# Filler from VectorE's zeros, batch 0's kv and raw products in halves, and a new order in an attention and gated-unit kernel

## The chip, the cores and the metric

The kernel runs on one core of a Trainium2 chip. The metric is the device time of one execution in microseconds; lower is better. A core has five engines with a queue each, and a queue runs in order: TensorE (PE, matrix products, with PEld for the loads of its stationary operand), VectorE (DVE), ScalarE (ACT), GpSimd (POOL) and SyncE (SP, which here only issues transfers). TensorE writes to PSUM, eight banks of 2 KB in each of 128 partitions; the other working memory is SBUF, and inputs and output lie in HBM, moved by 16 DMA engines. Steps on different engines are ordered by semaphores.

## The reference

Eight batches of linear attention (8 heads, 576 tokens, 64 wide) are followed by a gated unit with a causal convolution of five taps:

```python
kv = np.einsum('bhsd,bhse->bhde', k, v)
out = np.einsum('bhsd,bhde->bhse', q, kv)
rms = np.sqrt(np.mean(out * out, axis=-1, keepdims=True) + 1e-06)
out = out / rms * g_norm
x = out.transpose(0, 2, 1, 3).reshape(B, S, H * D)      # 8 x 576 x 512
for k in range(5):
    gate_pre += conv_w[k] * xp[:, k:k + S, :]            # xp: x with 4 rows of zeros ahead
gate = 1 / (1 + np.exp(-gate_pre))
return gate * (x @ w_val) @ w_out
```

q, k, v and `g_norm` are float32. The weights `w_val`, `conv_w` and `w_out` come as float64; the kernel reads them as pairs of 32-bit words and narrows them itself.

## The kernel before

**Plan and queues.** All work is cut into named steps (`kv_product 0 1` is half 1 of batch 0). A string, `PLAN`, holds some 1,235 of them in an order that a planner has written out; the program goes through it and issues each step's instructions, so the order of every engine's queue is the order of the plan, and so is SyncE's queue of transfers. Tiles come from pools: a PSUM bank is used again when its readers are done.

**Set-up.** `set_up` (L279) clears small tiles on VectorE (`warm`, biases, the whole of `kv_bd`) and makes the identity matrix on GpSimd (`make_identity`). `start_warm n` (L427) issues n filler products of 32 rows and columns, each of two instructions, that read the identity; nobody reads what they write.

**Batch 0 and 1, the opening.** Queries come in whole rows (`load_q_rows`, two transfers for a batch, one for each half of the heads), k and v in halves (`load_half`; batch 0's v on ScalarE's queue). `turn_q_rows b j` (L471) transposes four blocks of 32 tokens by products with the identity, and `sort_q` (L481) copies them from PSUM in the order of the heads. `kv_product b i` (L432) makes k'v for half i of the head pairs, 72 instructions of 64x64. For batch 0 alone `kv_copy` (L445) places the results as diagonal blocks in `kv_bd`, whose other blocks stay zero, so that a raw product `raw_whole 0 c` (L506) takes a chunk c of 128 tokens (chunk 4: 64) and two heads at once, 128x128. Its bank holds all four head pairs. Before, `kvps` of batch 0 is two banks, one for each s (the head within a pair's rows of k), both with two halves i; a copy step takes one bank and both halves, on ScalarE, and every raw product stands behind both copies.

**From raw to x.** `square` (ScalarE), `sums` (VectorE), `powers` (GpSimd, to the power -0.5) and `normalise` (batch 0: VectorE; others: ScalarE) give x; `turn_x` (TensorE) and `keep_x` (ScalarE), or from batch 2 on `turn_blocks` (VectorE) and `move_blocks` (transfers), transpose it into `xT`. `halo` (GpSimd) places the rows that the convolution needs.

**Gate, value, output.** `gate_start` (ScalarE), four `gate_tap` (VectorE), `gate_end` (ScalarE, sigmoid) and `gated` (VectorE) are the gate of one of four column blocks; `val_product`, or from batch 2 on `val_fast` with sums of blocks made ahead (seven products for eight), the value. `fast_product` does the same for the output matrix, with `token_sums` on VectorE; `out_product` takes the last 64 tokens of two batches at once. `store` writes the rows, `store_last` the last two blocks from two queues.

**Weights.** `stage_weight` loads float64 words; `narrow_weight name n part` has eight parts: 0, 5, 6, 4 and 7 on VectorE, 1, 2 and 3 on ScalarE. `cw`, the taps, is narrowed first, turned by `turn_cw` on TensorE and kept by `keep_cw`, whose `gcol` every `wval` needs in part 7. `warm_up` runs one sigmoid on ScalarE, which loads its table.

Of the kernel before, what the change touches and what calls it, by code (L numbers as in the profile page):

```python
# [15 lines left out]
P = 128  # L16
# [3 lines left out]
load_q_rows 0 1; stage_weight cw 0; load_q_rows 0 0; load_half v 0 0; load_half k 0 0; narrow_weight cw 0 5;  # L20
narrow_weight cw 0 6; narrow_weight cw 0 0; load_half v 0 1; load_half k 0 1; narrow_weight cw 0 1;
narrow_weight cw 0 2; warm_up; stage_weight wval 1; stage_weight wval 0; start_warm 36; turn_q_rows 0 3;
turn_q_rows 0 2; turn_q_rows 0 0; kv_product 0 0; turn_q_rows 0 1; sort_q 0 0; sort_q 0 1; narrow_weight cw 0 3;
narrow_weight cw 0 4; narrow_weight cw 0 7; turn_q_rows 0 4; turn_cw; keep_cw; kv_product 0 1; sort_q 0 4;
sort_q 0 3; kv_copy 0 0; kv_copy 0 1; narrow_weight wval 1 5; narrow_weight wval 1 0; sort_q 0 2; raw_whole 0 3;
load_q_rows 1 1; narrow_weight wval 1 1; narrow_weight wval 1 6; narrow_weight wval 1 2; raw_whole 0 4;
raw_whole 0 2; load_q_rows 1 0; narrow_weight wval 0 0; narrow_weight wval 0 5; square 0 3; stage_weight wval 3;
narrow_weight wval 0 6; narrow_weight wval 1 3; sums 0 3; load_half k 1 0; square 0 2; square 0 4;
narrow_weight wval 0 1; narrow_weight wval 1 4; sums 0 2; narrow_weight wval 0 2; raw_whole 0 0; raw_whole 0 1;
powers 0 3; sums 0 4; narrow_weight wval 1 7; normalise 0 3; square 0 1; square 0 0; sums 0 1; sums 0 0;  # L30
turn_q_rows 1 2; turn_q_rows 1 0; turn_q_rows 1 3; narrow_weight wval 0 3; sort_q 1 0; turn_x 0 3;
turn_q_rows 1 4; sort_q 1 2; turn_q_rows 1 1; keep_x 0 3; narrow_weight wval 3 0; load_half v 1 0;
stage_weight wval 2; load_half k 1 1; load_half v 1 1; powers 0 2; sort_q 1 3; normalise 0 2;
narrow_weight wval 3 1; narrow_weight wval 0 4; normalise 0 4; narrow_weight wval 0 7; narrow_weight wval 3 5;
stage_weight wout 1; load_q 2 0; stage_weight wout 0; powers 0 1; turn_x 0 4; narrow_weight wval 3 2;
turn_x 0 2; load_half k 2 0; kv_product 1 0; load_q 2 2; stage_weight wout 2; normalise 0 0; normalise 0 1;
narrow_weight wval 3 3; keep_x 0 2; keep_x 0 4; narrow_weight wval 3 4; narrow_weight wval 2 0; turn_x 0 0;
narrow_weight wval 3 6; turn_x 0 1; val_product 0 1 1; keep_x 0 0; kv_product 1 1; keep_x 0 1;
narrow_weight wval 3 7; narrow_weight wval 2 5; gate_start 0 0; val_product 0 3 1; gate_start 0 3;
narrow_weight wval 2 1; halo 0; sort_q 1 4; kv_copy 1 1; sort_q 1 1; kv_copy 1 0; gate_start 0 1;  # L40
narrow_weight wval 2 2; raw_pair 1 3; gate_tap 0 0 3; gate_tap 0 0 2; gate_tap 0 3 3; narrow_weight wval 2 3;
gate_tap 0 3 2; gate_tap 0 0 1; narrow_weight wout 1 0; narrow_weight wout 1 5; narrow_weight wval 2 6;
narrow_weight wval 2 4; load_half v 2 0; load_half k 2 1; load_q 2 1; square 1 3; narrow_weight wout 1 1;
narrow_weight wout 1 2; raw_tail 1; load_half v 2 1; keep_val 0 1 1; val_product 0 0 0; square 1 2;
narrow_weight wval 2 7; keep_val 0 3 1; gate_tap 0 3 1; sums 1 3; gate_tap 0 0 0; narrow_weight wout 0 0;
gate_tap 0 1 3; sums 1 2; turn_q 2 0; powers 1 3; keep_val 0 0 0; gate_end 0 0; val_product 0 2 1;
val_product 0 0 1; powers 1 2; load_q 2 3; narrow_weight wout 1 3; square 1 4; normalise 1 3; sums 1 4;
narrow_weight wout 1 6; narrow_weight wout 1 4; gate_tap 0 1 2; keep_val 0 0 1; val_product 0 1 0; raw_pair 1 1;
normalise 1 2; powers 1 4; turn_x 1 3; square 1 0; val_product 0 2 0; narrow_weight wout 1 7; gated 0 0;
gate_tap 0 1 1; keep_val 0 1 0; normalise 1 4; narrow_weight wout 0 1; sums 1 0; gate_start 0 2; turn_x 1 4;  # L50
turn_x 1 2; val_product 0 3 0; square 1 1; keep_x 1 4; keep_x 1 3; keep_x 1 2; narrow_weight wout 0 5;
gate_tap 0 3 0; val_sums 0; narrow_weight wout 2 5; narrow_weight wout 2 0; powers 1 0; gate_tap 0 2 3;
gate_tap 0 2 2; narrow_weight wout 0 2; gate_tap 0 2 1; sums 1 1; narrow_weight wout 0 3; keep_val 0 2 0;
keep_val 0 3 0; keep_val 0 2 1; stage_weight wout 3; narrow_weight wout 0 4; narrow_weight wout 0 6;
gate_tap 0 1 0; narrow_weight wout 2 6; gate_end 0 3; kv_product 2 0; normalise 1 0; powers 1 1;
val_product 1 0 1; halo 1; val_product 1 1 1; kv_product 2 1; turn_x 1 0; normalise 1 1; keep_val 1 0 1;
turn_q 2 2; narrow_weight wout 0 7; gate_tap 0 2 0; gate_end 0 1; gate_end 0 2; val_sums 1; turn_q 2 1;
gated 0 3; gated 0 2; turn_x 1 1; val_product 1 3 1; load_q 3 0; keep_x 1 0; turn_q 2 3; load_q 3 1;
load_half v 3 0; load_half v 3 1; narrow_weight wout 2 1; kv_copy 2 1; keep_x 1 1; weight_sums 0; val_sums 2;
gate_start 1 1; val_product 1 1 0; kv_copy 2 0; keep_val 1 1 1; narrow_weight wout 2 2; gate_tap 1 1 3;  # L60
keep_val 1 3 1; narrow_weight wout 2 3; narrow_weight wout 3 0; raw_pair 2 3; narrow_weight wout 3 5;
gate_tap 1 1 2; gated 0 1; square 2 2; square 2 3; keep_val 1 1 0; gate_start 1 0; narrow_weight wout 3 1;
raw_pair 2 1; val_product 1 0 0; narrow_weight wout 3 2; val_product 1 3 0; narrow_weight wout 3 3;
narrow_weight wout 3 6; token_sums 0 0 0; sums 2 3; val_product 1 2 1; val_product 1 2 0; powers 2 3; sums 2 2;
turn_q 3 0; token_sums 0 0 1; narrow_weight wout 3 4; square 2 1; keep_val 1 0 0; keep_val 1 3 0; load_q 3 3;
narrow_weight wout 3 7; narrow_weight wout 2 4; narrow_weight wout 2 7; load_half k 3 0; load_q 3 2;
load_half k 3 1; powers 2 2; fast_product 0 0 0; sums 2 1; normalise 2 3; token_sums 0 0 2; turn_blocks 2 3;
normalise 2 2; square 2 0; turn_q 3 1; powers 2 1; gate_start 1 3; fast_product 0 1 0; fast_product 0 0 1;
fast_keep 0 0 0; keep_val 1 2 0; normalise 2 1; weight_sums 1; raw_tail 2; sums 2 0; gate_tap 1 0 3;
fast_keep 0 0 1; fast_product 0 0 2; fast_keep 0 0 2; powers 2 0; square 2 4; keep_val 1 2 1; fast_keep 0 1 0;  # L70
weight_sums 2; token_sums 0 0 3; fast_product 0 0 3; fast_product 0 0 5; turn_blocks 2 2; turn_blocks 2 1;
sums 2 4; fast_keep 0 0 5; gate_tap 1 0 2; normalise 2 0; fast_product 0 0 4; fast_product 0 1 2; powers 2 4;
fast_keep 0 1 2; store 0 0; normalise 2 4; turn_blocks 2 0; move_blocks 2 0; move_blocks 2 2; move_blocks 2 1;
kv_product 3 0; fast_keep 0 0 4; turn_q 3 2; gate_tap 1 0 1; gate_tap 1 0 0; weight_sums 3; turn_q 3 3;
fast_product 0 1 4; turn_x 2 4; fast_product 0 1 1; kv_product 3 1; keep_x 2 4; kv_copy 3 0; kv_copy 3 1;
fast_product 0 0 6; move_blocks 2 3; raw_pair 3 3; raw_pair 3 1; gate_tap 1 3 3; load_half v 4 0; load_q 4 0;
gate_end 1 0; fast_keep 0 1 1; square 3 3; fast_keep 0 0 6; square 3 1; fast_product 0 1 3; fast_product 0 1 5;
gate_tap 1 3 2; gated 1 0; fast_keep 0 1 4; gate_tap 1 1 1; val_fast 2 0 0; sums 3 3; sums 3 1; gate_tap 1 1 0;
fast_keep 0 1 5; square 3 0; fast_product 0 1 6; square 3 2; sums 3 2; x_sums 2 0; gate_end 1 1; val_fast 2 1 0;
powers 3 3; x_sums 2 1; x_sums 2 3; gate_tap 1 3 1; gate_tap 1 3 0; val_fast 2 0 1; val_keep 2 0 0;  # L80
val_fast 2 0 2; x_sums 2 2; val_sums 3; sums 3 0; gated 1 1; fast_keep 0 1 6; val_keep 2 1 0; normalise 3 3;
val_keep 2 0 2; powers 3 2; powers 3 1; gate_end 1 3; val_fast 2 1 2; val_fast 2 1 1; load_half k 4 0;
val_keep 2 1 2; gate_start 1 2; val_keep 2 0 1; val_fast 2 0 4; gate_tap 1 2 3; val_keep 2 1 1; gate_tap 1 2 2;
val_fast 2 1 4; val_fast 2 0 5; val_fast 2 1 5; load_half v 4 1; normalise 3 2; load_half k 4 1; val_keep 2 0 4;
turn_blocks 3 2; val_keep 2 1 4; turn_q 4 0; val_keep 2 1 5; store 0 1; load_q 4 1; store 0 3; gate_tap 1 2 1;
# [122 lines left out]
def kernel(  # L208
# [11 lines left out]
    nc = tc.nc  # L220
# [628 lines left out]
```

## Time and profile before

| | |
|---|---|
| time, median of 3 runs | 306.39 us (304.39 to 307.18) |
| the profiled execution | 306.42 us |
| its span, first to last instruction | 304.6 us |
| TensorE busy | 294.8 us, 97% |
| VectorE busy | 269.2 us, 88% |
| ScalarE busy | 193.7 us, 64% |
| GpSimd busy | 114.9 us, 38% |
| mean granted clock of TensorE | 0.993 |
| moved by DMA | 55.53 MB, 182 GB/s in the mean |

All times below count from the first instruction of the span. A line such as L512 is a line of the kernel before. The granted clock is the share of TensorE's full clock that its throttle let through; its record starts 10.51 us into the span. The end of a product in a row is modelled and products overlap, so where rates matter the distance from one start to the next is used.

### The profile page before, as it was taken

What the parts mean: (1) busy time and instruction counts of PE and PEld (TensorE: products, weight loads), DVE (VectorE), ACT (ScalarE), POOL (GpSimd) and SP (SyncE); (2) the same over time, 40 slices, a digit from 0 to 9 for tenths busy, and PEclk for the clock granted to TensorE, in tenths of its full rate; (3) what the DMA queues carried; (4) which work ended last, traced back from release to release, by engine and by line L of the source; (5) the groups of instructions that cost most, each with busy time, mean ns of one, the idle gap of its engine ahead of it and who ended that gap; (6) DMA issues with size and microseconds to landing.
All of it is one profiled execution on the core that took longest, in us unless ns stands there. A gap on an engine that the chain in (4) does not pass through costs nothing.

```text
span 304.6 us, 8977 instructions
## 1 busy us (share of the span) xinstructions
PE 294.8 (97%) x3441; PEld 232.4 (76%) x3441; DVE 269.2 (88%) x474; ACT 193.7 (64%) x596; POOL 114.9 (38%) x127
## 2 busy tenths in 40 slices
PE   7899999999999999999999999999999999999993
PEld 7788778877787785777778757787878588888582
DVE  1169999999999999999999999999999999999612
ACT  1569989999768664884586547683787354535220
POOL 3027354406568217364338352345536631000000
PEclk9979999999999999999999999999999999999999
DMA  7999998088569756988689477927411621112423
GB/s 269 343 368 343 272 302 210 4 230 269 154 147 329 231 163 167 269 220 260 173 253 294 111 175 232 326 72 214 114 48 30 169 80 34 36 42 64 103 69 103
DMA packets 32074, 55.53 MB, mean 182 GB/s; under 512 B 6166, under 2 KB 14358, under 8 KB 32032
## 3 DMA queue, kind: packets, MB, share of 16 engines
q1 hardware_dynamic: 29520, 49.76, 55.7%
q0 software_dynamic: 1632, 3.17, 4.1%
q10 hardware_dynamic: 880, 2.03, 1.8%
q8 instruction: 27, 0.44, 0.6%
q14 instruction: 15, 0.12, 0.1%
HBM read 39.21 MB, written 9.44 MB: 160 GB/s over the span
## 4 chain that ended last, share of the span: by engine, by line
PE 89%; DVE 5%; DMA 2%; issue 1%; ACT 1%; DVEq 0%; ACTq 0%; SPq 0%
PE a L774 18%; PE cb L774 14%; PE va L682 13%; PE val L633 11%; PE vc L682 6%; PE kvps L440 6%; PE raw L501 5%; PE out L720 5%; PE vb L682 4%; PE qTps L477 4%; PE raw L512 2%; PE xTps L583 2%; DMA qs<-in_q_dram 2%; DVE gate L621 2%; DVE xs L667 1%
## 5 line engine op out<-in xcount | busy, mean ns | idle before, releaser
L552 POOL TENSOR_TENSOR rt<-ss,mhalf 128x8 f32<-128x8 f32 (+3 forms) x38 | 68.9, 1822 | 101.0 <-DVE ss L544 100.8
L621 DVE SCALAR_TENSOR_TENSOR gate<-xT,cwT,gate 128x576 f32<-128x576 f32 x128 | 101.8, 809 | 1.0
L571 ACT ACTIVATE x<-raw,rt 128x64 f32<-128x64 f32 x252 | 55.8, 351 | 7.2 <-POOL rt L552 4.2
L604 POOL DMA_DIRECT2D xT<-y x48 | 26.4, 557 | 25.5 <-DVE ot L784 14.0
L633 PE MATMUL val<-xT,wval 128*128 128x288 f32 x128 | 33.0, 411 | 0.0
L774 PE MATMUL a<-wsum,sums 128*128 128x256 f32 x128 | 32.4, 382 | 0.0
L628 ACT ACTIVATE gate<-gate 128x576 f32<-128x576 f32 x32 | 22.0, 692 | 11.7 <-DVE gate L621 11.4
L633 PEld LDWEIGHTS val<-xT,wval 128*128 128x128 f32 x128 | 23.5, 190 | 6.5 <-ACT xT L590 0.4
L544 DVE TENSOR_REDUCE ss<-sq 128x8 f32<-128x520 f32 (+1 forms) x40 | 24.7, 627 | 2.9 <-ACT sq L531 2.5
L774 PEld LDWEIGHTS a<-wsum,sums 128*128 128x128 f32 x128 | 24.0, 190 | 4.1 <-issue 0.6
L535 ACT ACTIVATE sq<-raw 128x256 f32<-128x256 f32 (+1 forms) x70 | 22.4, 403 | 7.3 <-PE raw L501 7.1
L682 PE MATMUL va<-xs,vsum 128*128 128x288 f32 x96 | 26.6, 409 | 0.0
L615 ACT ACTIVATE gate<-xT,cwT 128x576 f32<-128x576 f32 x32 | 25.2, 811 | 1.5 <-DVE gv L646 1.3
L646 DVE TENSOR_TENSOR gv<-gv,gate 128x576 f32<-128x576 f32 x32 | 23.6, 750 | 0.9 <-ACT gate L628 0.8
L682 PEld LDWEIGHTS va<-xs,vsum 128*128 128x128 f32 x96 | 18.0, 190 | 5.1 <-ACT x L571 0.4
L611 POOL COPY xT<-xT 128x124 f32<-128x124 f32 x32 | 17.5, 585 | 10.5 <-ACT xT L590 10.5
L501 PEld LDWEIGHTS raw<-kv,qT 64*64 64x64 f32 x1008 | 16.4, 134 | 5.3 <-issue 3.0
L440 PEld LDWEIGHTS kvps<-v,k 64*64 64x64 f32 x1008 | 15.9, 135 | 3.7 <-issue 1.9
L501 PE MATMUL raw<-kv,qT 64*64 64x64 f32 x1008 | 18.7, 221 | 0.0
L440 PE MATMUL kvps<-v,k 64*64 64x64 f32 x1008 | 17.6, 220 | 0.0
L774 PE MATMUL cb<-wsum,sums 128*128 128x256 f32 x64 | 16.9, 386 | 0.1
L774 PE MATMUL cb<-wout,gv 128*128 128x256 f32 x64 | 16.8, 385 | 0.0
(111 smaller groups left out, 542.3 us busy)
## 6 DMA issues: line engine op xcount, KB each, us to landing
qs<-in_q_dram SPq DMA_DIRECT2D x96, 140.0 KB, 4.2
out_dram<-ot SPq DMA_DIRECT2D x140, 64.0 KB, 1.7
k<-in_k_dram SPq DMA_DIRECT2D x14, 576.0 KB, 6.3
v<-in_v_dram SPq DMA_DIRECT2D x12, 576.0 KB, 6.5
xT<-y SPq DMA_DIRECT2D x48, 64.0 KB, 2.7
xT<-y POOLq DMA_DIRECT2D x48, 64.0 KB, 3.3
y<-in_moe_w_val_dram SPq DMA_DIRECT2D x4, 512.0 KB, 11.4
w_wout<-in_moe_w_out_dram SPq DMA_DIRECT2D x4, 512.0 KB, 6.3
```

The lines of the kernel that those rows point to most:

```text
L440: nc.tensor.matmul(st["kvps", b][s][r * D:(r + 1) * D, i], st["k", b, i][rows, r, cols], st["v", b, i][rows, r, cols], start=(j == 0), sto ...
L501: nc.tensor.matmul(st["raw", b, c][r][cols, to * D:(to + 1) * D], st["qT", b][rows, hp, first:first + D], kvs[b % 2][rows, hp, :], start=T ...
L544: nc.vector.reduce_sum(out=st["ss", b][:, FIRST[c]:FIRST[c] + n], in_=st["sq", b, c][:, 0:n], axis=AX.X)
L552: nc.gpsimd.tensor_tensor(out=st["rt", b][:, which], in0=st["ss", b][:, which], in1=mhalf[:, which], op=ALU.pow)
L571: nc.scalar.activation(out=x[:, to * D:(to + 1) * D], in_=raw[:, h * D:(h + 1) * D], func=AF.Copy, scale=root[:, to:to + 1])
L604: (nc.sync if i % 2 else nc.gpsimd).dma_start(out=xTs[b % 2][i * TB:(i + 1) * TB, :, first:first + P], in_=y[a * TB:(a + 1) * TB, i])
L615: nc.scalar.activation(out=gate[:], in_=xTs[b % 2][:, jt, HALO:SX], func=AF.Copy, scale=cwT[:, K - 1, jt:jt + 1])
L621: nc.vector.scalar_tensor_tensor(out=gate[:], in0=xTs[b % 2][:, jt, tap * TB:tap * TB + S], scalar=cwT[:, tap, jt:jt + 1], in1=gate[:], op ...
L633: nc.tensor.matmul(val[:], wval[:, kc, jt * P:(jt + 1) * P], xTs[b % 2][:, kc, HALO + n * SV:HALO + (n + 1) * SV], start=(kc == 0), stop=( ...
L646: nc.vector.tensor_tensor(out=both, in0=both, in1=st["gate", b, jt][:], op=ALU.mult)
L682: nc.tensor.matmul(st[bank, "val", b, mj][:], weights_[:, k], tokens()[:, k], start=(n in (0, 1, 3) and k == 0), stop=(k == NK // 2 - 1), ...
L774: nc.tensor.matmul(st[bank, i, p], tokens()[:, k], weights_[:, k], start=(n < 2 and k == 0), stop=(k == NK // 2 - 1), skip_group_check=True)
```

## The change

1. `set_up` clears the first 32 columns of `kv_bd` as VectorE's very first instruction and the rest of it later; `start_warm` reads those zeros instead of the identity, and the plan asks for 50 products (100 instructions) instead of 36 (72).
2. For batch 0, `kv_product` writes each half i and each s to a bank of its own: four banks instead of two. `kv_copy 0 n` copies half n alone, in four pieces of 64x64: the upper 64 partitions on ScalarE, the lower on VectorE. Before, a step made two pieces of 64x128 on ScalarE.
3. `raw_whole b c i` runs the two head pairs of half i alone, so that a half can run before the other half's kv is there. The products are the same in number and size.
4. The whole plan is new. Its opening, by name: the exponent of `cw` (part 0) is taken first and its part 3 stands right behind `warm_up`; TensorE runs query blocks 4, 0, 3, then kv half 0, query block 1, raw half 0 of chunk 3, `turn_cw`, query block 2, kv half 1, raw half 0 of chunk 2, and then the other raw halves; `load_q_rows 1` stands behind query block 2 (before: behind block 1, ahead of block 4); the `wval` narrowing on VectorE starts behind `kv_copy 0 1`.

```diff
     def set_up():
+        nc.vector.memset(kv_bd[:, 0, 0:TB], 0.0)
         nc.vector.memset(warm[:], 0.0)
...
         make_identity(nc, ident[:])
-        nc.vector.memset(kv_bd[:], 0.0)
+        nc.vector.memset(kv_bd[:, 0, TB:], 0.0)
+        nc.vector.memset(kv_bd[:, 1:], 0.0)
...
     def start_warm(n):
         for _ in range(n):
-            nc.tensor.matmul(warm_bank()[0:TB, 0, 0:TB], ident[:, 0:TB], ident[:, 0:TB], start=True, stop=True)
+            nc.tensor.matmul(warm_bank()[0:TB, 0, 0:TB], kv_bd[:, 0, 0:TB], kv_bd[:, 0, 0:TB], start=True, stop=True)
...
         if ("kvps", b) not in st:
-            st["kvps", b] = [ps([P, 2, D], f"kvps{b}_{s}") for s in range(2)]
+            whole = b in WHOLE
+            banks = [ps([P, 2 - whole, D], f"kvps{b}_{n}") for n in range(4 if whole else 2)]
+            st["kvps", b] = [[banks[2 * i + s][:, 0] if whole else banks[s][:, i] for i in range(2)] for s in range(2)]
+            st["kvbanks", b] = banks
...
-    def kv_copy(b, s):
-        ps_ = st["kvps", b][s]
+    def kv_copy(b, n):
         if b in WHOLE:
             for r in range(2):
                 rows = slice(r * D, (r + 1) * D)
-                nc.scalar.copy(
-                    out=kv_bd[rows, :, rows].rearrange("p (i s) e -> p s i e", s=2)[:, s], in_=ps_[rows])
+                for s in range(2):
+                    to, ps_ = kv_bd[rows, 2 * n + s, rows], st["kvps", b][s][n][rows]
+                    (nc.vector.tensor_copy if r else nc.scalar.copy)(out=to, in_=ps_)
             return
...
-    def raw_whole(b, c):
+    def raw_whole(b, c, i):
         m = size(c)
-        st["raw", b, c] = raw = ps([P, C if c < NJ else C // 2], f"raw{b}_{c}")
-        for hp in range(HP):
+        if ("raw", b, c) not in st:
+            st["raw", b, c] = ps([P, C if c < NJ else C // 2], f"raw{b}_{c}")
+        for hp in (2 * i, 2 * i + 1):
```

The plan before, its opening up to the second raw product (loads left out):

```
narrow_weight cw 0 5; narrow_weight cw 0 6; narrow_weight cw 0 0; narrow_weight cw 0 1; narrow_weight cw 0 2; warm_up;
start_warm 36; turn_q_rows 0 3; turn_q_rows 0 2; turn_q_rows 0 0; kv_product 0 0; turn_q_rows 0 1; sort_q 0 0;
sort_q 0 1; narrow_weight cw 0 3; narrow_weight cw 0 4; narrow_weight cw 0 7; turn_q_rows 0 4; turn_cw; keep_cw;
kv_product 0 1; sort_q 0 4; sort_q 0 3; kv_copy 0 0; kv_copy 0 1; narrow_weight wval 1 5; narrow_weight wval 1 0;
sort_q 0 2; raw_whole 0 3; ...; raw_whole 0 4; raw_whole 0 2
```

The plan after, the same stretch:

```
narrow_weight cw 0 0; narrow_weight cw 0 5; narrow_weight cw 0 1; narrow_weight cw 0 2; warm_up; narrow_weight cw 0 3;
start_warm 50; turn_q_rows 0 4; turn_q_rows 0 0; turn_q_rows 0 3; kv_product 0 0; turn_q_rows 0 1;
narrow_weight cw 0 6; narrow_weight cw 0 4; sort_q 0 0; sort_q 0 3; kv_copy 0 0; narrow_weight cw 0 7;
raw_whole 0 3 0; turn_cw; turn_q_rows 0 2; sort_q 0 2; keep_cw; kv_product 0 1; raw_whole 0 2 0; sort_q 0 4;
load_q_rows 1 0; load_q_rows 1 1; sort_q 0 1; kv_copy 0 1; narrow_weight wval 1 5; narrow_weight wval 1 0;
narrow_weight wval 1 6; raw_whole 0 3 1; raw_whole 0 4 0; raw_whole 0 4 1; raw_whole 0 2 1
```

## The prediction

> **What bounds the kernel now.** I read the page first, then the busy time by stretches, then TensorE's own row of time through the opening.
>
> The first part of the page and the stretches (columns: busy microseconds and instructions of TensorE, its weight loads, VectorE, ScalarE, GpSimd; granted clock; DMA share; GB/s):
>
> ```profile
> PE 294.8 (97%) x3441; PEld 232.4 (76%) x3441; DVE 269.2 (88%) x474; ACT 193.7 (64%) x596; POOL 114.9 (38%) x127
> ```
> ```profile
> 14.00:17.30 3.30, 1.69 (x74) 1.55 (x75) 2.49 (x9) 1.75 (x7) 0.00 (x0) 1.00 0.76 249
> 17.30:20.80 3.50, 3.50 (x18) 2.74 (x19) 1.91 (x5) 3.36 (x7) 0.00 (x0) 0.51 1.01 374
> ...
> 30.00:210.00 180.00, 179.36 (x2389) 139.26 (x2381) 178.51 (x307) 132.41 (x436) 82.40 (x89) 1.00 0.74 212
> 210.00:280.00 70.00, 69.79 (x506) 55.38 (x505) 67.27 (x109) 38.12 (x114) 22.48 (x27) 1.00 0.29 77
> ```
> Two engines are full from 30 to 280 us: TensorE is idle 0.85 us there, VectorE 1.49 + 2.73 us. So an opening that is shorter for one engine alone is worth nothing, and a re-planned middle has almost nothing left to win and all of that to lose. TensorE's order in time through the opening (start, length, line, product, count, idle before and its releaser):
>
> ```profile
> 1.36 4.05 PE L430 MATMUL warm<-ident 128*32 128x32 f32 x72 [1.36 <-POOL ident masks.py:199]
> 6.12 5.05 PE L477 MATMUL qTps<-ident,qs 128*64 128x128 f32 x48 [0.70 <-DMA qs<-in_q_dram]
> 11.10 1.28 PE L440 MATMUL kvps<-v,k 64*64 64x64 f32 x72
> 12.31 1.53 PE L477 MATMUL qTps<-ident,qs 128*64 128x128 f32 x24
> 15.05 0.21 PE L414 MATMUL cwps<-ident,cw 21*128 21x21 f32 x1 [1.22 <-issue]
> 15.19 1.40 PE L440 MATMUL kvps<-v,k 64*64 64x64 f32 x72
> 17.15 6.32 PE L512 MATMUL raw<-kvbd,qT 128*128 128x128 f32 x40 [0.56 <-ACT kvbd L450]
> 23.40 2.84 PE L477 MATMUL qTps<-ident,qs 128*64 128x128 f32 x48
> ```
> The same 48 query products take 105 ns each at 6.12 and 59 ns at 23.40: the clock was at half before 10.51, where its record begins (the stretches print 1.00 where there is no record). It fell to half once more, from 17.34 to 20.75, behind the idle 1.22 and 0.56 us: a stretch of 3.41 us that was busy 1.7 us, some 49%. The 40 raw products cost 6.25 us from start to start; the full-rate ones among them are 0.11 us apart, so 4.42 would do, and 1.83 us is the clock. Between 6.12 and 23.40 TensorE has 11.2 us of work at the full rate (72 query, 144 kv, 40 raw products): 6.1 us is there to be had.
>
> **The change part by part.**
>
> *Filler.* 72 instructions in 4.05 us are 54 ns each; 100 last 5.4. They wait for VectorE's first clear (first row at 0.81, some 0.06 long), not for GpSimd's identity at 1.36: from 0.95 to 6.3. The queries land at 6.07 and 6.25, so the 0.70 us gap closes and the work behind it is not delayed. Worth in time: nothing by itself, because of what follows. With the clock up early, the 40 query products (8 fewer now ahead of the first kv product) end at 8.7 and kv waits for its values, which land at 9.49; with it low they end at 10.5. kv half 0 and the query block behind it (1.21 + 0.94) end at 11.65 or 12.65. Both are too early for ScalarE:
>
> *ScalarE to the first kv copy.* The exponent of `cw` is taken first (L363 at 8.45, not 8.90), so its chain runs 0.45 earlier: two steps to 9.5, the table load 1.28 to 10.8, the sigmoid, the third step of `cw` to 11.4 (before it stood behind a query sort and ended at 14.33), two sorts (0.57 long, 0.48 apart) to 12.45, then the copies. A kv copy was 64x128 at 0.26; a 64x64 has no row, so its bounds are half of that, 0.13, and 0.26; I take 0.25, as a 21-column read of the same memory on VectorE (L419, 128x20) still took 0.24. VectorE's half has the same 0.25, bounds 0.15 and 0.41 (its 128x256 copy L797), and stands behind ScalarE's copy of the same bank. All four end at 13.2. All bounds move this by 0.5 either way.
>
> *First raw half and the rest.* Raw half 0 of chunk 3 runs at 13.2 for 0.44; `turn_cw` finds its input ready at 13.45 (not 15.02): 13.8; query block 2 to 14.75; kv half 1 (landed 13.80) to 15.95; raw half 0 of chunk 2 to 16.4. The second copies follow ScalarE's three sorts: 16.9. The other 32 raw instructions at 0.11 end at 20.5, against 23.40: 2.9 us for TensorE, 1.8 of it the clock. Splitting the raw products adds none.
>
> *What is queued behind.* On VectorE the first weight narrowing stood at 15.84; now it stands behind the second kv copies at 16.9. But from 15.84 to its first gate step at 33.11 it was idle 2.85 us (1.56 and 0.90 for squares, the rest in small pieces), so 14.4 us of work; the squares now come about 2 us earlier, and with no such wait the first gate step is at 31.3: 1.8 us earlier. On SyncE the batch 1 queries are now issued behind query block 2, 14.75 against 13.88, and with them nine transfers (two queries, four halves of k and v, two `wval`, one `wout`) some 0.85 later. Queries then land at 18.5 and 20.0 (were 17.61, 19.18), covered by 0.5 us; the first k and v halves of batch 1 at 26.3, needed at 27.2: covered.
>
> *TensorE to the first value product.* Two query blocks to 22.4; `turn_x 0 3` waits for its normalised chunk until 22.9 (sums 18.85, power 2.06, then six VectorE steps); the next query block waits for a bank that ScalarE frees behind three `wval` steps (0.7 each), until 24.65. From there rows of before: blocks 1.88, two turns 0.65, kv 1.21, block 0.47, two turns 0.95: the first value product at 29.85, against 31.16. So 1.3 us arrives on TensorE, 1.8 on VectorE.
>
> *The tail* has the same chain: the last product, a copy of 0.42, a store. Behind the last whole-bank product TensorE has 14 product steps of 0.86 us, before 13; the order ahead of it is one shorter, so the sum is unchanged unless VectorE is late there.
>
> Sum: the profiled execution took 306.42 us, its span 304.6; 306.42 - 1.3 = **305.1 us**. The median of the three runs shown is 306.39, so nothing is shifted.
>
> [...]
>
> **The rivals.**
>
> *The clock falls in a new wait (chance 0.22).* If the filler does lift the clock, TensorE idles from 11.65 to 13.2, and 10.51 to 13.93 is busy only 55%; from 20.75 to 24.17 it idles 0.5 and 0.8, 62%. Against it: 49% is the only share that is known to have dropped it, and the first stretches of filler, busy 68% and 79%, were low already. One fall in the first place makes 13.93 to 17.34 slow: query block and kv half 1 take 2.15 more, less the wait that this covers, some 1.2 late for both engines: 306.3. In the second, TensorE loses 1.5: 306.6.
>
> *VectorE late at the last batch (0.18, slower).* The place: `gated 7 0`, on which the last whole-bank product waits. Before, the gated rows ended at 283.77 and that product began at 284.41. Now TensorE would be there at 284.41 - 0.86 - 1.3 = 282.25, VectorE at 283.77 - 1.8 = 281.97, if its queue meets only the idle that it meets now. Each microsecond more than 0.28 is a microsecond of the end; slower than before from 1.6. If a wholly new order meets the idle of 30 to 280 us (4.2) twice: 306.42 - 1.3 + 3.9 = 309.0. For it: full engines and a strange order; against it: the counts of instructions are the same, and VectorE still has idle time after 210.
>
> *All of it arrives (0.20).* The whole 2.9 us of TensorE survives, because later waits fill behind stages that have slack: 303.5, and with luck in the middle 303. Against: VectorE gains 1.8 at best.
>
> *No filler effect at all* gives the forecast too, as shown.
>
> **How the numbers follow.** Forecast 305.1 with 0.40, between 304.2 and 306; clock 306.3 to 306.6 with 0.22; all arrives 303.5 with 0.20, half of it under 303.3; VectorE late 309.0 with 0.18, half of it above. One per cent is 3.06 us, which is also the spread of the runs shown (304.39 to 307.18) and about what a measurement can tell. So faster 0.10, same 0.81, slower 0.09. The range 303.0 to 308.7 leaves out about half of the last case and a third of the one before.
>
> **What would show it.** Filler from 0.95 to 6.3 and no gap before the query products; first raw product near 13.2, the last ending near 20.5 at 0.11 us spacing; the first weight narrowing near 16.9; the first value product near 29.9 and gate step near 31.3; no half clock between 14 and 27; VectorE idle 30 to 210 still under 2 us. Wrong it is if the clock drops again, if kv copies take over 0.4 us, or if VectorE idles in the middle.

## The result: 3.3% slower, and where the profile after has the time

The kernel after takes 315.75 us (median of 4 runs, 313.34 to 317.44); the kernel before, on the same chip, 305.39 us (304.08 to 307.18). The ratio is 1.0329, with a 95% interval of 1.0232 to 1.0426. The prediction was 305.1 us, the same within 1%, and its range ended at 308.7. It was wrong.

The profiled execution after took 313.34 us, the shortest of the four; its span is 311.6 us, 7.0 us more than the one before (304.6 us). The first part of its page, and the same stretches that were shown of the kernel before:

```profile
PE 296.5 (95%) x3469; PEld 233.5 (75%) x3469; DVE 270.0 (87%) x480; ACT 192.3 (62%) x596; POOL 113.5 (36%) x127
```
```profile
14.00:17.30 3.30, 3.30 (x96) 2.89 (x96) 1.29 (x7) 1.55 (x5) 0.00 (x0) 1.00 0.47 139
17.30:20.80 3.50, 3.50 (x36) 3.09 (x37) 3.47 (x9) 3.18 (x6) 1.78 (x1) 1.00 1.01 374
30.00:210.00 180.00, 173.78 (x2247) 135.19 (x2246) 170.49 (x292) 126.71 (x419) 78.81 (x81) 0.98 0.71 205
210.00:280.00 70.00, 69.50 (x582) 54.26 (x581) 66.72 (x108) 38.60 (x123) 23.44 (x30) 1.00 0.32 85
```

The two stretches of the opening have become what they were meant to be: TensorE busy throughout, at the full clock. The loss is in the third. There TensorE is idle 6.22 us (before 0.64) and VectorE 9.51 us (before 1.49). TensorE's own row of time through the opening:

```profile
0.96 5.32 PE L434 MATMUL warm<-kvbd 128*32 128x32 f32 x100 [0.96 <-DVE kvbd L282]
6.28 2.40 PE L486 MATMUL qTps<-ident,qs 128*64 128x128 f32 x40
10.84 1.28 PE L447 MATMUL kvps<-v,k 64*64 64x64 f32 x72 [2.16 <-DMA k<-in_k_dram]
12.05 1.09 PE L486 MATMUL qTps<-ident,qs 128*64 128x128 f32 x16
13.07 0.71 PE L522 MATMUL raw<-kvbd,qT 128*128 128x128 f32 x4
...
16.12 4.42 PE L522 MATMUL raw<-kvbd,qT 128*128 128x128 f32 x36
20.47 1.97 PE L486 MATMUL qTps<-ident,qs 128*64 128x128 f32 x32
23.20 0.66 PE L593 MATMUL xTps<-ident,x 128*128 128x128 f32 x4 [0.77 <-DVE x L571]
```

The 40 query products take 60 ns each: the clock was already up. The raw products run at their full rate, and the first value product starts at 29.22 us instead of 31.16. So after 30 us the new kernel was 1.94 us ahead, and it ended 7.0 us behind: some 9 us went in the middle. The waits of TensorE name two places (columns: waiting instruction, what it waited for, us in total, times, longest):

```profile
PE raw L510 <- issue: 3.0, 1, 3.0
PE va L692 <- DVE ot L794: 2.7, 1, 2.7
```

The first has no semaphore behind it: "issue" is time in which the engine waited for nothing that the profile shows. TensorE's row of time around it, then the stretches around it:

```profile
58.81 0.68 PE L593 MATMUL xTps<-ident,x 128*128 128x128 f32 x4
59.42 2.15 PE L510 MATMUL raw<-kv,qT 64*64 64x64 f32 x124
64.61 0.48 PE L510 MATMUL raw<-kv,qT 64*64 64x64 f32 x4 [3.04 <-issue]
```
```profile
56.00:61.50 5.50, 5.50 (x141) 4.54 (x139) 5.43 (x12) 4.77 (x16) 1.32 (x1) 1.00 0.71 210
61.50:64.60 3.10, 0.07 (x2) 0.00 (x0) 3.06 (x7) 2.03 (x6) 0.85 (x1) 0.88 1.02 266
64.60:70.70 6.10, 6.09 (x16) 4.40 (x17) 6.07 (x11) 4.56 (x13) 5.99 (x4) 0.50 0.98 292
```

TensorE stands still for 3.04 us four products before the end of a run of 128 raw products, and it is not waiting for data: the same kv and the same bank were good enough for the product before. The DMA engines are full (share 1.02), and one packet among theirs is of another kind than all the rest:

```profile
q1 hardware_dynamic: 309, 0.81, 99.2%
q8 instruction: 1, 0.02, 2.4%
```

These are the queues of 61.5 to 64.6 us. The page of the whole execution has 27 such instruction packets with 0.44 MB, so 16.3 KB each, and TensorE has 2 x 3469 = 6938 instructions (a weight load and a product each): 257 for a packet. The packet in the stand-still runs from 62.03 to 63.21 us, and TensorE goes on 1.40 us later. Here a block of TensorE's program came late.

It costs more than 3.04 us. From 63.84 to 70.67 us the granted clock is at half. The kernel before has the same two runs at the full clock:

```profile
63.76 2.09 PE L501 MATMUL raw<-kv,qT 64*64 64x64 f32 x128
65.79 8.03 PE L633 MATMUL val<-xT,wval 128*128 128x288 f32 x32
73.65 1.67 PE L774 MATMUL a<-wout,gv 128*128 128x256 f32 x7
```

From start to start the raw products take 5.59 us after and 2.03 before, the 32 value products behind them 10.64 and 7.86: 3.57 us for the stand-still with the four slow products behind it, and another 2.78 for the clock. In 70 to 83 us VectorE idles 1.18, 1.99 and 1.87 us, each time until ScalarE has normalised the rows that it is to transpose.

The second place is near 130 us. The value product `val_fast 3 1 0` needs a PSUM bank that `fast_keep 0 3 5` empties, and that keep stands in VectorE's queue behind two gate taps (`gate_tap 2 2 3` and `gate_tap 2 3 1`) that wait for nobody: VectorE is simply full.

```profile
131.33 1.50 DVE L631 SCALAR_TENSOR_TENSOR gate<-xT,cwT,gate 128x576 f32<-128x576 f32 x2
132.75 0.68 DVE L794 TENSOR_TENSOR ot<-cb,ot 128x512 f32<-128x512 f32 x1
```

By start-to-start times TensorE loses 3.57 + 2.78 us at the first place and 2.88 at the second, 9.2 in all; less the 1.94 gained this is 7.3, and the spans differ by 7.0. So two theories were to be tested: that the loss belongs wholly to the new order behind the opening, and that its largest part is a matter of where a block of instructions ends.

### The profile page after: what moved, and what is told of

It reads as the page before. It is cut to its first block, busy times and chain, and to the rows that moved or that the text cites. A ratio compares the mean times of both kernels' runs of the same rounds, so it can differ in the third digit from the quotient of the medians.

```text
span 311.6 us, 9042 instructions
## 1 busy us (share of the span) xinstructions
PE 296.5 (95%) x3469; PEld 233.5 (75%) x3469; DVE 270.0 (87%) x480; ACT 192.3 (62%) x596; POOL 113.5 (36%) x127
## 3 DMA queue, kind: packets, MB, share of 16 engines
q10 hardware_dynamic: 880, 2.03, 1.8%
## 4 chain that ended last, share of the span: by engine, by line
PE 78%; DVE 10%; DMA 5%; SPq 4%; issue 2%; ACT 1%; DVEq 0%; ACTq 0%
PE a L784 16%; PE va L692 11%; PE cb L784 11%; PE val L643 11%; PE kvps L447 6%; PE vc L692 6%; PE raw L510 5%; DVE gate L631 4%; DMA k<-in_k_dram 3%; PE vb L692 3%; PE out L730 2%; PE qTps L486 2%; SPq L816 2%; PE xTps L593 2%; DVE xs L677 2%
## 5 line engine op out<-in xcount | busy, mean ns | idle before, releaser
L614 POOL DMA_DIRECT2D xT<-y x48 | 26.6, 559 | 31.9 <-DVE sums L762 11.6
L643 PE MATMUL val<-xT,wval 128*128 128x288 f32 x128 | 35.7, 436 | 0.0
L784 PE MATMUL a<-wsum,sums 128*128 128x256 f32 x128 | 33.1, 384 | 0.2 <-DVE sums L762 0.2
L545 ACT ACTIVATE sq<-raw 128x256 f32<-128x256 f32 (+1 forms) x70 | 21.7, 383 | 16.6 <-PE raw L510 16.4
L643 PEld LDWEIGHTS val<-xT,wval 128*128 128x128 f32 x128 | 25.5, 204 | 7.3
L692 PE MATMUL va<-xs,vsum 128*128 128x288 f32 x96 | 27.6, 412 | 0.5 <-DVE xs L677 0.3
L510 PEld LDWEIGHTS raw<-kv,qT 64*64 64x64 f32 x1008 | 16.9, 135 | 8.7 <-issue 6.5
L510 PE MATMUL raw<-kv,qT 64*64 64x64 f32 x1008 | 19.4, 222 | 3.0 <-issue 3.0
L606 DVE STREAM_TRANSPOSE y<-x 128x512 f32<-128x512 f32 x24 | 16.7, 701 | 5.0 <-ACT x L581 5.0
L621 POOL COPY xT<-xT 128x124 f32<-128x124 f32 x32 | 16.4, 551 | 7.8 <-DMA xT<-y 5.9
L784 PE MATMUL a<-wout,gv 128*128 128x256 f32 x64 | 16.8, 389 | 0.0
```

Of the source, the lines that this page charges most:

```text
L510: nc.tensor.matmul(st["raw", b, c][r][cols, to * D:(to + 1) * D], st["qT", b][rows, hp, first:first + D], kvs[b % 2][rows, hp, :], start=T ...
L614: (nc.sync if i % 2 else nc.gpsimd).dma_start(out=xTs[b % 2][i * TB:(i + 1) * TB, :, first:first + P], in_=y[a * TB:(a + 1) * TB, i])
L643: nc.tensor.matmul(val[:], wval[:, kc, jt * P:(jt + 1) * P], xTs[b % 2][:, kc, HALO + n * SV:HALO + (n + 1) * SV], start=(kc == 0), stop=( ...
L692: nc.tensor.matmul(st[bank, "val", b, mj][:], weights_[:, k], tokens()[:, k], start=(n in (0, 1, 3) and k == 0), stop=(k == NK // 2 - 1), ...
L784: nc.tensor.matmul(st[bank, i, p], tokens()[:, k], weights_[:, k], start=(n < 2 and k == 0), stop=(k == NK // 2 - 1), skip_group_check=True)
```

## The experiments

None of these kernels leaves work out: filler products are read by nobody, and all else is computed as before. Each kernel's rows have line numbers of its own.

**The same kernel once more.** No edit.

> The changed kernel once more, unaltered, for a second profile. In its first profile TensorE stood still from 61.6 to 64.6 us, inside a run of 128 raw products with no semaphore to wait for, while a 16 KB block of its instructions was being fetched (62.03 to 63.21), and the clock was at half for 6.8 us behind it. If the late fetch is the cause (theory F), a stall of 1 to 4 us inside some run of raw or kv products is there again, not necessarily the same one, with a fetch in it, and the time is 312 to 318 us. If the new order itself is (theory O: TensorE runs ahead of VectorE and SyncE's queue in the middle), the stalls of TensorE have VectorE or a transfer as their releaser, at the same steps as in the first profile.

It took 315.2 us. The stand-still is there again, at the same instruction:

```profile
60.91 2.15 PE L510 MATMUL raw<-kv,qT 64*64 64x64 f32 x124
66.37 0.33 PE L510 MATMUL raw<-kv,qT 64*64 64x64 f32 x4 [3.31 <-issue]
```

The 2.7 us wait near 130 is there as well. Both have to do with the program, not with one execution. The clock, however, differs: this time it was at half from 12.14 to 15.55 us as well, behind a wait of 2.16 us for k that ends at 10.78, and the first value product came at 30.77 us. Behind the wait near 130 it fell too (135.02 to 138.43), which it had not done before.

**Each half of the new plan with the other half of the old one.** The first kernel has all edits and the new order up to the first value product, and then the order of before; the second has the code and the order of before up to that order's own first value product, and then the new order.

```
 first:   new plan up to "val_product 0 0 1", then every step not yet issued in the order of before
 second:  old plan up to "val_product 0 1 1", then every step not yet issued in the new order
```

> The changed kernel's code, with the new order up to the first value product and the order of before from there. If the loss lies in the new middle (theories F and O), this keeps the opening's 1.3 to 1.9 us and loses nothing: 303 to 305 us against 305.4. If the new opening is what upsets the later stages (theory S: TensorE comes early, VectorE does not), 309 or more. By F a chance remains that a fetch falls badly here too: then 306 to 309 with a stall inside a run of short products.

> The code of before and its order up to the first value product, the new order from there. By O the whole loss is here, and the opening's gain is not: 315 to 318 us. By S nothing is lost: 305 to 307. By F the blocks of instructions begin elsewhere than in the changed kernel (28 fewer filler instructions), so the stall of 61.6 is moved or gone: 306 to 313, by where it falls.

New opening, old rest: 305.61 us against 304.53, ratio 1.0026 (0.9990 to 1.0062). Old opening, new rest: 316.4 us, ratio 1.0342 (1.0268 to 1.0417). The loss is in the order behind the opening, and the opening, which had looked some 1.9 us faster in the profile, is worth nothing that can be measured.

The second of these lost its time in part in other places than the kernel after, so that the two totals are alike is chance. Its waits:

```profile
PE val L617 <- ACT qT L468: 3.6, 1, 3.6
PE va L666 <- DVE ot L768: 2.7, 1, 2.7
PE vc L666 <- ACT gv L677: 1.9, 1, 1.9
```

The 3.6 us, from 37.6 to 41.3 us, come from the seam between the two orders and are no part of the change. The 2.7 is the bank of the kernel after. The 1.9, near 199 us, is new: in ScalarE's queue `normalise 6 2`, which waits for GpSimd's root, stands ahead of `val_keep 5 1 1`, which would empty the bank that TensorE needs. Each of the three was followed by 3.41 us at half clock. The stand-still at 60 us is missing here, so this run alone doesn't say what it is worth.

**The filler alone.** The plan of before, with 50 products on VectorE's zeros.

```diff
-start_warm 36
+start_warm 50
```

> The kernel before with part 1 alone: zeros of VectorE, 50 products. The forecast has this at nothing, as kv waits for its transfer and ScalarE: 304.5 to 306.5. If an early full clock is worth something by itself, 303 to 304; if the filler makes TensorE late or the clock falls in a longer wait, 307.

306.04 us, ratio 1.0047 (1.0017 to 1.0077): if anything slower. In its profile the clock's record starts at 6.87 us instead of 10.51. Over all profiles it starts at 4.74 to 6.87 us in the six with 50 filler products and at 5.53 to 10.51 in the four with 36, so with 50 the clock was up by 6.87 us each time, and with 36 not always; but here it then fell at 17.11, behind the same waits of 1.22 and 0.63 us as in the kernel before, and for 6.83 us instead of 3.41.

**The late block of instructions.** Every filler product is four TensorE instructions, two products and two weight loads, so taking some away moves all later instructions against the blocks and leaves their order alone: 30 or 14 fewer shift them by 120 or 56 down, 14 more by 56 up.

```diff
-start_warm 50
+start_warm 20      (the others: 36, 64)
```

> The changed kernel with 20 filler products instead of 50: 120 instructions of TensorE fewer at the start, the order untouched. In both profiles of the changed kernel the 3.0 and 3.3 us stall came at the same instruction, at the end of a run of 256 short instructions that fills one 16 KB block of TensorE's instructions almost exactly, behind two full loads that SyncE had just issued. Theory F: with the blocks shifted by 120 the run spans two blocks, the stall (3 us) and the half clock behind it (1.7 to 3.4 us of work) are gone: 309 to 311 us, no idle of TensorE over 0.5 us between 58 and 70. Theory O (the order alone, filler and blocks do not matter): the stall stays and the time is 313 to 317.

> The kernel after with 36 filler products instead of 50: 56 TensorE instructions fewer ahead of everything, as against 120 in the run with 20. Theory 1, the late instruction block: its place against the run of 128 short raw products near 62 us is what counts, and this shift, too, moves it away, to within 14 instructions of where the kernel before has it; no stand-still over 0.6 us at 58 to 70 us, no half clock there, 309 to 310.5 us. Rival, the length of the filler itself or the load of the DMA queues near 60 us: the stand-still of some 3 us and the half clock behind it are still there, 313 to 316 us.

> The kernel after with 64 filler products instead of 50: 56 TensorE instructions more ahead of everything. Theory 1, the place of an instruction block: in the kernel after the block that came late begins with the 2242nd TensorE instruction, the run of 128 short raw products is instructions 1993 to 2248, so the run uses up the whole block before it in 2.2 us. Shifted by 56 the run is 2049 to 2304, only 192 of its instructions lie before that block and some 6 us of slow value products ahead of them give the transfer time: no stand-still over 1 us at 58 to 70 us, no half clock there, 308 to 311 us (0.8 to 1.5 of it the longer filler). Rival, a long filler as such: stand-still and half clock as in the kernel after, or worse, 314 to 317 us.

| filler products | shift | us | ratio to before (95%) | stand-still at 58 to 70 us |
|---|---|---|---|---|
| 50 (the kernel after) | 0 | 315.75 | 1.0329 (1.0232 to 1.0426) | 3.04, then half clock for 6.83 us |
| 20 | -120 | 309.40 | 1.0154 (1.0031 to 1.0277) | none |
| 36 | -56 | 307.99 | 1.0093 (1.0057 to 1.0130) | none |
| 64 | +56 | 310.53 | 1.0204 (1.0147 to 1.0261) | none |

The kernels with 20 and 64 were timed twice each, the one with 36 eight times.

The same run of 128 raw products with 64 filler products, the longest filler of all:

```profile
60.05 2.10 PE L493 MATMUL raw<-kv,qT 64*64 64x64 f32 x128
62.07 8.03 PE L626 MATMUL val<-xT,wval 128*128 128x288 f32 x32
```

So a longer or a shorter filler removes the stand-still alike: it is the place of the run, not the filler's length, and by the ratios it costs some 4 to 7 us. The other two waits stayed, and the three kernels print them alike:

```profile
PE va L675 <- DVE ot L777: 2.7, 1, 2.7
PE vc L675 <- ACT gv L686: 1.8, 1, 1.8
```

**The bank near 130 us.** The keep step goes ahead of the two gate taps.

```diff
+fast_keep 0 3 5
 gate_tap 2 2 3
 gate_tap 2 3 1
-fast_keep 0 3 5
```

> The changed kernel with one step of VectorE, fast_keep 0 3 5, moved ahead of two gate taps (of gate blocks 2 and 3 of batch 2); nothing else. In three profiles of the new order TensorE stood 2.7 us near 131 until this step freed its PSUM bank, behind two gate taps. Theory O: the wait shrinks by 1.4 us to about 1.3, no half clock follows it, and the time falls by 1 to 3 us to 312 to 314. If VectorE is simply full there (the wait is only a shift), the time stays at 314 to 316 and VectorE is late by as much elsewhere.

> Both of the other two edits. If the loss is the late fetch and the bank's wait together, with what the clock adds to each (F and O, additive): 306 to 309 us. If other waits of the new order take their place: 310 to 313.

With 50 filler products 313.16 us (ratio 1.0277, 1.0141 to 1.0414), with 20 of them 309.19 us (1.0147, 1.0043 to 1.0250). The wait shrank from 2.7 to 1.3 and 1.1 us. The first kernel takes 2.6 us less than the kernel after did on another chip (1.6 us by the ratios), inside the spread of two timed executions; in the second the edit brought nothing: the wait at 192 us was still there, the clock fell behind it (194.98 to 198.40), and a run of raw products at 35 us now stood still for 1.5 us with "issue" behind it. Two timed executions each don't settle a microsecond, so the next kernel took all of the waits away at once.

**All three repairs.** 36 filler products, the keep moved as above, the value product that needs its bank behind one more output product, and the normalising step behind the keep steps. Steps that stand between those shown are left out.

```diff
-start_warm 50
+start_warm 36
...
-normalise 6 2
 val_keep 5 1 1
 val_keep 5 0 1
+normalise 6 2
...
-val_fast 3 1 0
-val_keep 3 1 0
 fast_product 0 3 4
+val_fast 3 1 0
+val_keep 3 1 0
```

> The kernel after with 36 filler products and the three waits of the new order that its traces and those of its variants named moved away, nothing left out: one keep step on VectorE ahead of two gate taps, the value product that waits for that keep's bank one product step later on TensorE (both near 128 us), and the normalising step on ScalarE behind two keep steps instead of ahead of them (near 192 us). Theory: the named waits and the half clocks behind them are the whole loss; 304 to 306.5 us, within 1% of before. Rival: a wholly new order waits in many small places, and where one wait goes the next comes up; 308 us or more, with new waits over 1 us on TensorE that the runs so far did not show.

304.37 us against 305.87, ratio 0.9962 (0.9925 to 0.9998): all of the loss is gone, and within 1% the kernel is the same as the one before. The first part of its page, its middle stretch, and the longest waits of TensorE:

```profile
PE 291.7 (96%) x3441; PEld 230.3 (76%) x3441; DVE 269.6 (89%) x480; ACT 192.1 (63%) x596; POOL 115.5 (38%) x127
```
```profile
30.00:210.00 180.00, 177.60 (x2360) 138.88 (x2359) 177.05 (x306) 130.11 (x434) 83.41 (x84) 1.00 0.74 211
```
```profile
PE qTps L469 <- DMA qs<-in_q_dram: 1.8, 2, 1.5
PE a L767 <- DVE gv L639: 1.0, 1, 1.0
PE warm L417 <- DVE kvbd L265: 1.0, 1, 1.0
```

Behind the opening one wait of 1.0 us is left, and the granted clock is whole from 5.53 us to the end of TensorE's work. Next to the run with 36 filler products on the same chip (307.99), the two moved waits are worth 3.6 us; in that run they had cost 2.7 + 1.8.

**The repairs, but with the block as it was.** The same kernel with 50 filler products.

> The kernel with the three moved waits, but with 50 filler products again, as the kernel after has them; nothing left out. Theory 1: the run of short raw products stands against its instruction blocks as in the kernel after, so the stand-still of some 3 us at 61 to 65 us and the half clock behind it come back: 309 to 312 us, 5 to 7 us above the same kernel with 36. Rival, the stand-still needed the late stages of the kernel after: no stand-still, 304 to 306 us.

Its two executions took 316.36 (the profiled one) and 310.62 us, too far apart for a ratio; the kernel before takes 304.29 on that chip. The profiled one stands still at the same instruction, and for longer:

```profile
61.01 2.15 PE L493 MATMUL raw<-kv,qT 64*64 64x64 f32 x124
68.94 0.48 PE L493 MATMUL raw<-kv,qT 64*64 64x64 f32 x4 [5.78 <-issue]
```

Its instruction packet ran from 66.25 to 67.48, 1.46 us ahead of TensorE; the wait ahead of the packet is what grew. The half clock behind it lasts from 66.18 to 73.01. Even the shorter execution is 2.1% above the kernel before, where the same kernel with 36 was 0.4% below: 14 filler products that nobody reads, with everything else well ordered, cost some 7 us. In the profiled execution some 2 us more lie in the opening, where the clock fell as in the second execution of the kernel after.

## Why the prediction was wrong, step by step

**What bounds the kernel: right, and not used.** The text says that a re-planned middle "has almost nothing left to win and all of that to lose". The sum then carried the middle over at nothing. That is the step that failed: the sum, 306.42 - 1.3, has a term for the opening (-1.3) and one for the tail (0), and none for some 1,100 steps in a new order. In the profiled execution that term measured +9.2 us on TensorE, in three pieces: 3.57 at the stand-still, 2.78 of half clock behind it, 2.88 for a bank. The -1.3 failed too: it measured nothing (1.0026; below, under Arrivals).

**The rival on the slower side: right in kind, wrong in place and in size.** It expected a new order to meet the idle time of 30 to 280 us twice (+3.9), at `gated 7 0`, the last batch. No wait is found there: from 270 to 300 us TensorE is busy without a gap. The waits came near 130 us, at a value product whose bank VectorE empties late, and in most variants near 192 us as well. Without the late block the rival is close in size: 309.4, 308.0 and 310.5 us with 20, 36 and 64 filler products, against its 309.0. As place and wait were others, that is in part luck.

**The late block: in no rival.** The prediction asked of the filler what it does to TensorE's time and clock. It also moves the program, by 56 instructions, and with the new order that run of 128 raw products, 256 instructions, came to fill one block of TensorE's program almost exactly. What is shown is that the stand-still comes in all four profiles with 50 products and this order, always before the same four products, and in none of the profiles where the shift is -120, -56 or +56; and that a 16 KB instruction packet lies in it.

How the delay comes about can be read from the same traces. Count TensorE's records in order of time, loads, products and semaphore instructions alike: in all four profiles it stands still before record 2242. In the thirteen profiles there are ten waits of TensorE over 0.45 us named "issue", apart from that of `turn_cw` for its input. They come before records 450, 1218 (twice), 1730, 1986, 2242 (four times) and 3010, all of them 194 above a multiple of 256, and each ends 1.33 to 1.58 us after an instruction packet. So these places are read here as the block boundaries.

In these profiles the packets that came late came with the DMA engines loaded. Of the first nine packets of each profile, 112 of 117 start after TensorE has entered the block ahead of the one that they bring, up to 6.0 us after. The 69 that start over 2 us after had the engines at a share of 0.84 or more until then; the 19 with a share under 0.6 came within 2 us. No run changed the load alone.

What such a lateness costs went with the length of the block ahead. In the kernel after TensorE enters the block ahead at 58.81, has done with it in 2.76 us, and the packet starts 3.22 us after the entry. With 36 filler products the packet is nearly as late, 2.71 us after the entry at 59.15, with the engines as full; but there the block ahead holds value products and lasts 7.73 us.

**The filler: right.** It ran from 0.96 to 6.28 us (predicted 0.95 to 6.3), the gap closed, and alone it is worth nothing, as said: 1.0047.

**The first raw product: right to 0.13 us, by luck.** It came at 13.07 us (predicted 13.2), but not by the path of the sum. The sum let kv wait for its values, at 9.49 us, and had ScalarE's chain end last. In the trace kv waits 2.16 us for k and starts at 10.84, and from there TensorE works without a gap through kv half 0 and the query block to 13.07. The copies were done by 12.77, so the later landing of k, not ScalarE's chain, set the first raw product.

**The copies: right.** 0.22 us for a 64x64 piece on VectorE and 0.21 on ScalarE (taken: 0.25). The raw products ended at 20.47 us (20.5), the wait of `turn_x` was 0.77 (to 23.20; predicted 22.9), and the first weight narrowing began at 16.93 (16.9).

**Arrivals.** First value product 29.22 us (predicted 29.85), first gate step 32.05 (31.3). Both are within 0.8; the wait for a bank until 24.65 was not there, as the query block began at 23.79. But the comparison with before was made against an unlucky execution. Its clock fell in the opening and cost 1.83 us, and the prediction counted that as won. The same opening of before had, in the run with the new rest, its clock up from 7.13 us, and reached its first value product at 28.66 us. The new opening reached it at 28.63, 28.67, 29.17, 29.22, 29.31, 29.50, 29.53, 30.77, 30.85 and 30.88 us in ten profiles. There is no gain in these numbers, and the 10 executions of the new opening with the old rest (1.0026) say the same.

**The clock falling in a new wait: right as a mechanism, another wait.** The rival had TensorE idle from 11.65 to 13.2 us and the clock at half from 13.93. That idle time is not there; the wait for k, from 8.7 to 10.8, is. The clock did not fall in the profiled execution; in three others (the kernel again, new opening with old rest, the repairs with 50 products) it was at half from 12.1, 12.3 and 11.6 us for 3.41 us, and the first value product came some 1.6 us later. The price was 1.2 to 1.5 us, so its size was fair; it was not what decided.

**The gap ahead of half clock.** The prediction names waits of 1.22 and 0.56 us ahead of one fall. In the runs the wait of 2.7 us near 130 us was followed by half clock in four profiles of six (the kernel again, 20 and 64 products, and old opening with new rest), not in the kernel after nor with 36; the wait of 1.8 to 1.9 near 192 us in two of five. The same program, in two executions, met the same 2.7 us wait with and without a fall. So the length of the gap alone does not decide, and what does is not shown: no run set it.

## What to carry to other kernels

A new order for a part of a kernel that is full on two engines is a cost until each queue has been read through: put a term for it into the sum, and look for steps that empty a bank and stand behind work that waits for nobody, or behind a step that waits itself. A wait named "issue" inside a run of short instructions, with an instruction packet in it, was here a matter of where the run lies in the program. With 120 or 56 instructions fewer or 56 more ahead of it the 3.04 us were gone, with at most smaller waits elsewhere (0.60 and 0.91 us with 64 filler products), and 56 more ahead of the kernel with the three repairs brought on 5.78 us; so look for it again after an edit that adds instructions. And before a gain is read from one profiled execution, see whether its own clock had fallen there.

## What the runs showed of the hardware

- TensorE stood still for its own program for 3.04, 3.31, 3.04 and 5.78 us at one place, each time until 1.40 to 1.46 us after the end of a 16 KB instruction packet that took 1.05 to 1.27 us itself, and for 0.5 to 1.5 us six times elsewhere. All ten lie a multiple of 256 records of TensorE apart, or at the same record.
- The packet of a block started after TensorE had entered the block ahead of it in 112 of the 117 cases counted above, 3.2 to 5.8 us after the entry at those four, with the DMA engines at a share of 0.94 to 1.03 in between.
- The stand-stills of 3.04 us in the first profile and of 5.78 us each had 6.83 us of half clock with them, which nearly doubled the price in the first profile (3.57 and 2.78 us).
- A stretch of 3.41 us at half clock followed the gap of 2.7 us in four profiles of six and that of 1.8 to 1.9 us in two of five.
